# Top-k attention and a leaky-ReLU MLP on one core: the written order of a two-step cycle laid out anew

## The chip, the cores and the metric

The kernel runs on one core of a Trainium2 chip. The metric is the time of one execution in microseconds on the device. TensorE is called PE here, VectorE DVE, ScalarE ACT, GpSimd POOL, and SyncE, which issues most DMAs, SP.

## What is computed

q, k and v are (8, 8, 576, 64) in float32, x is what attention gives, as (4608, 512), w_in is (512, 2048) and w_out (2048, 512).

```python
scores = scale * np.matmul(q, k.transpose(0, 1, 3, 2))
kth = np.partition(scores, -top_k, axis=-1)[..., -top_k:-top_k + 1]   # top_k = 32
scores = np.where(scores >= kth, scores, -1000000000.0)
scores = scores - np.max(scores, axis=-1, keepdims=True)
attn = np.exp(scores)
attn = attn / (np.sum(attn, axis=-1, keepdims=True) + 1e-09)
x = np.matmul(attn, v)             # then (B, H, S, D) to (B*S, H*D)
h = x @ w_in
out = np.maximum(0.01 * h, h) @ w_out
```

## The kernel before

**Units.** Two heads share the 128 partitions, so 64 heads are 32 pairs. A unit is 128 rows of scores for two heads: 128 queries of one pair, or the 64 queries that 576 leaves over, of two pairs. There are 144 units, 18 for each batch. One step of the main loop (L742) begins one unit; two units that follow each other have their scores and their values computed together, in even steps.

**What a unit goes through.** `scores` (L214) multiplies 64x64 tiles on PE into PSUM tiles `wide` (two buffers) and `narrow`, and ACT copies them to `s_sb`. `top_k` (L295) is DVE's work: larger and smaller halves (`pairs`, L302), then four rounds of the eight largest (L307) with three replacements (L312) between; it is a generator that stops at each `yield`, and `slot()` lets it go on. `limits` (L316) makes `nleast` on ACT and `nbias` in two small POOL instructions. `mask` (L326) and `exponents` (L330) are two ACT passes each, `sums` a small ACT instruction that gives `ze`, `reciprocals` (L338) one on DVE that gives `rz`, and `normalize` (L342) two ACT passes more. `transpose` (L345) splits the float32 words into 16-bit halves on POOL (L352, two copies), sends them to DRAM (L353) and reads them back transposed as `wT` (L355), both on SP's queue. The first units and units 14 and 15, called HASTY, are transposed on PE instead (`transpose_in_haste`, L357, and ACT's copies in `keep_transposed`, L368). `weigh_whole` (L385) and `weigh_left` (L401) multiply `wT` with `vt` on PE, and `keep_values` (L413) copies the result to `x`, two copies per unit pair.

**The MLP** is another generator (`mlp`, L491). It takes the tokens in chunks of 256 (two of 128 at first, done by `plain`, L573). For one chunk PE computes eight times a `ph` of two blocks (L510, eight products in all), and ACT makes `gT` of each (L516). The second layer is a 2x2 block product of seven products (L524, L526), eight matmuls each. Some of these read sums that POOL makes (L467): after the fourth and the eighth `ph` three sums are put on a list (s1, s2 and one in g21), and `sum_now` issues what is on the list:

```python
            if f0 % 4 == 3:
                at = slice(f0 - 3, f0 + 1)
                sum_later(s1[:, at, :], g21[:, at, :], g22[:, at, :], ALU.add)
                sum_later(s2[:, at, :], s1[:, at, :], g11[:, at, :], ALU.subtract)
                sum_later(g21[:, at, :], g11[:, at, :], g21[:, at, :], ALU.subtract)
```

The products come in the order g11, g12, s2, s1, g21, g12 again, g22. `keep_sum` (L531) copies each finished sum from PSUM to `o_sb` on ACT, with six buffers. Between the second and the third product `mlp` calls `sum_now()` itself for all that is still on the list.

**What sets the order.** Everything is written in the order of the program, and each engine works in that order; a wait at the head of an engine's queue holds all behind it. `mlp_steps(budget)` lets the MLP's generator go on for so many columns of matmul; `slot_budget` (L648) spreads what is left of a chunk over the steps until the next chunk is ready, with seven such slots a step. A chunk is ready when `attended` is called, after the values of its last unit.

In an even step s the old order is: limits of unit s-1, transpose of unit s-2, mask with a slot between, exponents with `values` (units s-4 and s-3) between the two, the copies of x, `sum_now(3)`, slots, reciprocal and normalize of unit s-1, slots, `scores` of units s+2 and s+3 with their copies, a last slot. The odd step is the same without values and scores. A unit has its top-k in step n, softmax in step n+1, its transpose in step n+2; the pair's values come in step n+4 for even n (`values_at`, L622; one step earlier for HASTY).

Twelve units (26, 27, 34, 35 and the same 36 and 72 later) have their scores computed in the first steps, while PE has little else to do (`score_early`, L668, `EARLY_SCORES`), and kept in DRAM; their even steps have no `scores`.

Of the kernel before, what the change touches and what calls it, by code (L numbers as in the profile page):

```python
# [20 lines left out]
def kernel(  # L21
# [192 lines left out]
    def scores(us):  # L214


        narrow = ps_sc.tile([P, 2, 512], F32, name="narrow")
        ps = {}
        for k, u in enumerate(us):
            wide = ps_sc.tile([P, 2, 512], F32, name="wide", bufs=2)  # L220
            ps[u] = ((wide[:, :, 0:WIDE], 0, WIDE),
                     (narrow[:, :, k * NARROW:(k + 1) * NARROW], WIDE, S))

        order = ((us[0], 0), (us[0], 1), (us[1], 1), (us[1], 0))
        for u, part in order:
            to, k0, k1 = ps[u][part]
            for n in range(0, len(u.quarters), 4):
                for i, pi, side, r0, q0 in u.quarters[n:n + 4]:
                    qt, kt = qk_of[pi]
                    d = slice(side * D, (side + 1) * D)  # L230
                    nc.tensor.matmul(to[r0:r0 + LEFT, i, :], qt[d, q0:q0 + LEFT],  # L231
                                     kt[d, k0:k1], start=True, stop=True)
        for u in us:
            u.both = work.tile([P, 2, S], F32, name="s_sb", bufs=5)
            u.s = [u.both[:, i, :] for i in range(2)]
        for u, part in order:
            to, k0, k1 = ps[u][part]
            nc.scalar.copy(u.both[:, :, k0:k1], to)  # L238
# [106 lines left out]
    def transpose(u):  # L345


        pairs = u.both.rearrange("p i n -> p (i n)").bitcast(U16).rearrange("p (n h) -> p n h", h=2)
        apart = halves.tile([P, 2, 2 * S], U16, name="apart")
        for h in range(2):  # L350
            split = work.tile([P, 2 * S], U16, name="split", bufs=2)
            nc.gpsimd.tensor_copy(split, pairs[:, :, h])  # L352
            nc.sync.dma_start(apart[:, h, :], split)  # L353
        u.wT = work.tile([P, 2 * NKC - 1, P], F32, name="wT", bufs=3)
        nc.sync.dma_start_transpose(out=u.wT.bitcast(U16), in_=apart.rearrange("p h n -> (p h) n"))  # L355
# [57 lines left out]
    def keep_values(pair, po, b, q0):  # L413
        ch, col = x_at(b * S + q0)
        if ch not in x_of:
            x_of[ch] = [xpool.tile([P, CHMAX], F32, name=f"x{c}") for c in range(HP)]
        for side in range(2):
            nc.scalar.copy(x_of[ch][pair % HP + side][:, col:col + po.shape[-1]], po[:, side, :])  # L418
# [6 lines left out]
    def hidden_of_few(ch, x):  # L425

        g_of = {}
        for j in range(NFC // 4):
            ph = ps_ml.tile([P, 512], F32, name="ph", tag="ml")
            for c in range(HP):  # L430
                nc.tensor.matmul(ph, x[c][:, 0:P], w_in[c][:, j * 512:(j + 1) * 512],  # L431
                                 start=(c == 0), stop=(c == HP - 1))
                if c == 1:
                    yield 2 * 512
            g_of[j] = raws.tile([P, 2 * DMODEL], U16, name="scale", bufs=2).bitcast(F32)
            nc.scalar.activation(g_of[j], ph, AF.Prelu, alpha=SLOPE)
            yield 2 * 512
            if j:
                yield from turned(j - 1, g_of)
        few[ch] = g_of  # L440
# [50 lines left out]
    def mlp(ch):  # L491
# [13 lines left out]
        for f0 in range(HALF):  # L505
            ph = ps_ml.tile([P, 2, CHMAX], F32, name="ph", tag="ml")
            for i in range(2):
                f = f0 + i * HALF
                for c in range(HP):
                    nc.tensor.matmul(  # L510
                        ph[:, i, 0:n], w_in[c][:, f * P:(f + 1) * P], x[c][:, 0:n],
                        start=(c == 0), stop=(c == HP - 1),
                    )
                    if c == 1 or i == 0 and c == HP - 1:
                        yield 2 * n
# [102 lines left out]
    LAG = 3  # L618
    HASTY = (*range(8), 14, 15)
    MIDDLE, END = 0, 1  # L620

    def values_at(n):  # L622

        return (n | 1) + LAG - (n in HASTY), MIDDLE

# [3 lines left out]
    EARLY_SCORES = {0: 4, 1: 2, 2: 1, 3: 2, 4: 1, 5: 2}  # L629
# [5 lines left out]
    for n, u in enumerate(steps):  # L635
        ch, _ = x_at(u.b * S + u.q0)
        done_tokens[ch] += u.rows * len(u.pairs)
        if done_tokens[ch] == CHUNKS[ch] * HP:
            ready_at.append((values_at(n), ch))
    assert [ch for _, ch in ready_at] == list(range(len(CHUNKS)))  # L640

    def attended(*place):
        for at, ch in ready_at:
            if at == place:
# [3 lines left out]
    def slot_budget(s):  # L648

        after = [at for (at, _), _ in ready_at if at >= s]  # L650
        until = after[0] if after else s
        if len(after) >= len(CHUNKS) - EARLY:
            return EARLY_SHARE
        return backlog[0] / ((until + 1 - s) * SLOTS)

    EARLY_SHARE = 500
    SLOTS = 7

    with tc.manual_schedule():
# [15 lines left out]
        def load_more(s):  # L675

            at_once = 2
            while len(v_of) < NPAIR:
                n = len(v_of)
                due = values_at(starts[n])[0]  # L680
                if n < LOADED_V:
                    load_v(n)
                elif values_at(last[n - LOADED_V])[0] > s:
# [41 lines left out]
        def values(*place):  # L725
            due = [u for n, u in enumerate(steps) if values_at(n) == place]
            if not due:
                return ()
            po = ps_sc.tile([P, 2, 512], F32, name="wide", bufs=2)
            if len(due[0].pairs) == 1:  # L730
                weigh_whole(due, po, FULL + [QUARTERS])
                return [(due[0], po[:, :, 0:P])]
            for n, u in enumerate(due):
                weigh_left(u, po[:, :, n * LEFT:(n + 1) * LEFT])
            return [(u, po[:, :, n * LEFT:(n + 1) * LEFT]) for n, u in enumerate(due)]

        def keep(weighed, *place):
            for u, po in weighed:
                keep_values(u.pairs[0], po, u.b, u.q0)
            attended(*place)  # L740

        for s in range(len(steps) + LAG + 1):  # L742
            assert s < 7 or not to_keep
            cur, old, older, new = unit(s), unit(s - 1), unit(s - 2), ()
            in_haste = s - 2 in HASTY
            if s % 2 == 0:
                new = [u for u in steps[s + 2:s + 4] if u]
            if new and new[0] in early_units:
                new = ()
            picks = top_k(cur) if cur else iter(())  # L750
            budget = slot_budget(s)

            def slot():
                next(picks, None)

            slot()
# [4 lines left out]
            if older and not in_haste:  # L761
                transpose(older)
            if old:
                mask(old, 0)
            mlp_steps(budget)
            if older and in_haste:
                transpose_in_haste(older)
            if old:
                mask(old, 1)
            slot()  # L770
            if older and in_haste:
                keep_transposed(older)
# [3 lines left out]
            weighed = values(s, MIDDLE)  # L776
            if old:
                exponents(old, 1)
                sums(old)
            keep(weighed, s, MIDDLE)  # L780
# [4 lines left out]
            slot()  # L785
            if s % 2:
                slot()
            if old:
                reciprocals(old)
            mlp_steps(budget)  # L790
            if old:
                normalize(old, 0)
                normalize(old, 1)
            mlp_steps(budget)
            slot()
            slot()
            if unit(s + 3) in early_units:
                fetch_scores(unit(s + 3))
            mlp_steps(budget)
            if new:  # L800
                scores(new)
            score_early(EARLY_SCORES.get(s, 0))
            budget = slot_budget(s + 1)
            mlp_steps(budget)
            load_more(s)
        mlp_steps(1e9)
# [62 lines left out]
```

## Time and profile before

| what | us |
|---|---|
| median of 3 runs | 1463.82 (1461.76 to 1465.31) |
| the profiled execution | 1463.53 |
| its span in the profile | 1461.8 |
| mean granted clock of PE | 0.982 |
| PE, DVE, ACT, POOL busy in 300 to 1300, a mean 100 us | 97.4, 97.4, 74.6, 55.4 |
| DVE's first pairs row of a unit | 60.69 |
| DVE's last one | 1371.90 |

Durations of single instructions are the means of the profile's groups, or rows of its timeline, which merges instructions of one kind that follow each other (x is how many). In a list of waits the columns are: engine, what waited, for whom; the total in us, how often, the longest in us. A timeline row has its start, its duration, engine, line and operation, and in brackets the engine's idle time before it with what ended it. Instructions on PE are pipelined: the mean of one is longer than the distance between two.

The first 100 us convert the weights, which arrive as 64-bit floats. From about 400 us on PE works almost without a pause, and after DVE's last unit at 1381 PE still has the end of one MLP chunk and the whole of the last one.

### The profile page before, as it was taken

Reading aid. Unit: us, or ns where it says so; the run is one execution under the profiler, and the core shown is the slowest. Engines: PE = TensorE matmul, PEld = TensorE weight load, DVE = VectorE, ACT = ScalarE, POOL = GpSimd, SP = SyncE. Lnnn points to the kernel's source line nnn. Section 1 sums busy time; section 2 is a strip of 40 time slices with the busy share of each in tenths; the row PEclk is TensorE's granted clock in tenths of the full one; section 3 lists DMA queues with packets and bytes.
Section 4 is the critical chain, followed back from the end, with each engine's and each line's share of the span. In section 5 each row is a group of like instructions: output and inputs, shape, how many; then the busy total and the mean of one; then the engine's idle time right before and its main releaser. Section 6 shows DMA issues by size and latency. Waiting matters only on the chain.

```text
span 1461.8 us, 27967 instructions
## 1 busy us (share of the span) xinstructions
PE 1373.3 (94%) x9848; PEld 1065.6 (73%) x9850; DVE 1317.9 (90%) x3401; ACT 1058.5 (72%) x2235; POOL 728.6 (50%) x775
## 2 busy tenths in 40 slices
PE   7858988789999999999999999999899999999998
PEld 2335446668787788878788877778788888788887
DVE  7987899999999999999999999999899999999700
ACT  8887777668687878777778786768587877777711
POOL 3213333554646465555556564556465655555622
PEclk9989998999999999999999999999999999999999
DMA  8941154655666546664766557755766455545420
GB/s 328 343 163 50 57 137 117 180 166 141 198 171 173 141 135 190 189 175 137 211 167 180 145 143 190 190 161 151 191 168 174 130 165 143 164 138 145 131 63 15
DMA packets 384445, 232.19 MB, mean 159 GB/s; under 512 B 320944, under 2 KB 331696, under 8 KB 382384
## 3 DMA queue, kind: packets, MB, share of 16 engines
q1 hardware_dynamic: 383728, 229.88, 55.7%
q8 instruction: 77, 1.26, 0.4%
q14 instruction: 64, 0.52, 0.1%
q10 hardware_dynamic: 576, 0.52, 0.1%
HBM read 55.77 MB, written 95.55 MB: 104 GB/s over the span
## 4 chain that ended last, share of the span: by engine, by line
PE 65%; DVE 18%; DMA 7%; ACT 6%; issue 2%; POOL 2%; SPq 0%; ACTq 0%; DVEq 0%; POOLq 0%
PE ph L510 23%; PE pz L526 22%; PE wide L394 9%; DVE tops L307 8%; DVE pairs L312 6%; PE wide L231 4%; DMA wT<-apart 4%; PE narrow L231 2%; PE pz L578 2%; DVE pairs L302 2%; DMA apart<-split 2%; ACT s_sb L238 1%; PE ph L431 1%; DMA vt<-in_vk_dram 1%; ACT s_sb L331 1%
## 5 line engine op out<-in xcount | busy, mean ns | idle before, releaser
L307 DVE MAX8 tops<-pairs 128x8 f32<-128x288 f32 (+1 forms) x1152 | 638.5, 595 | 0.0
L510 PE MATMUL ph<-x,w_in 128*128 128x256 f32 x2176 | 491.7, 383 | 1.6 <-ACT gT L516 1.6
L510 PEld LDWEIGHTS ph<-x,w_in 128*128 128x128 f32 x2176 | 407.4, 190 | 84.0 <-issue 20.8
L312 DVE MATCH_REPLACE8 pairs<-tops,pairs 128x288 f32<-128x288 f32 (+1 forms) x864 | 461.5, 541 | 0.0
L323 POOL TENSOR_TENSOR nbias<-tops 128x2 f32<-128x2 f32 x144 | 107.9, 749 | 574.5 <-DVE tops L307 567.1
L352 POOL COPY split<-s_sb 128x1152 uint16<-128x1152 uint16 x268 | 298.7, 1143 | 8.3 <-ACT s_sb L343 8.3
L343 ACT ACTIVATE s_sb<-s_sb,rz 128x576 f32<-128x576 f32 x288 | 207.3, 768 | 66.9 <-DVE rz L340 66.7
L526 PE MATMUL pz<-w_out,gT 128*128 128x256 f32 x1088 | 245.2, 381 | 0.6 <-ACT o_sb L533 0.6
L526 PEld LDWEIGHTS pz<-w_out,gT 128*128 128x128 f32 x1088 | 205.7, 190 | 31.5 <-issue 2.5
L331 ACT ACTIVATE s_sb<-s_sb,nbias 128x576 f32<-128x576 f32 x288 | 219.3, 764 | 0.9
L328 ACT ACTIVATE s_sb<-s_sb,nleast 128x576 f32<-128x576 f32 x288 | 214.4, 770 | 4.7
L302 DVE TENSOR_TENSOR pairs<-s_sb 128x576 f32<-128x576 f32 x288 | 212.3, 778 | 5.0
L394 PE MATMUL wide<-wT,vt 128*64 128x128 f32 (+1 forms) x2560 | 165.4, 290 | 30.2 <-DMA wT<-apart 21.5
L394 PEld LDWEIGHTS wide<-wT,vt 128*64 128x64 f32 (+1 forms) x2560 | 134.6, 141 | 68.1 <-issue 31.3
L238 ACT COPY s_sb<-wide 128x704 f32<-128x704 f32 x130 | 98.1, 755 | 86.4 <-PE wide L231 86.4
L516 ACT ACTIVATE gT<-ph 128x512 f32<-128x512 f32 x136 | 80.5, 592 | 76.7 <-PE ph L510 76.7
L526 PE MATMUL pz<-raw,top 128*128 128x256 f32 x544 | 125.0, 384 | 0.0
L526 PEld LDWEIGHTS pz<-raw,top 128*128 128x128 f32 x544 | 101.1, 190 | 21.2 <-issue 8.4
L231 PE MATMUL wide<-kt,qt 64*64 64x352 f32 x1040 | 105.0, 474 | 3.6 <-ACT wT L371 2.9
L324 POOL TENSOR_SCALAR nbias<-nbias 128x2 f32<-128x2 f32 x144 | 85.8, 596 | 12.6
L418 ACT COPY x<-wide 128x128 f32<-128x128 f32 (+1 forms) x160 | 32.2, 260 | 74.4 <-PE wide L394 57.9
L533 ACT COPY o_sb<-pz 128x256 f32<-128x256 f32 x119 | 43.8, 368 | 57.1 <-PE pz L526 57.1
(81 smaller groups left out, 1202.1 us busy)
## 6 DMA issues: line engine op xcount, KB each, us to landing
apart<-split SPq DMA_DIRECT2D x268, 288.0 KB, 2.2
raw<-in_weights_dram SPq DMA_DIRECT2D x15, 1024.0 KB, 6.9
vt<-in_vk_dram SPq DMA_DIRECT2D x32, 320.0 KB, 3.9
qt<-in_qT_dram SPq DMA_DIRECT2D x32, 288.0 KB, 3.8
kt<-in_kT_dram SPq DMA_DIRECT2D x32, 288.0 KB, 3.9
out_dram<-o_sb SPq DMA_DIRECT2D x68, 128.0 KB, 3.0
kept<-gT SPq DMA_DIRECT2D x12, 576.0 KB, 4.3
s_sb<-kept SPq DMA_DIRECT2D x12, 576.0 KB, 4.3
```

The lines of the kernel that those rows point to most:

```text
L231: nc.tensor.matmul(to[r0:r0 + LEFT, i, :], qt[d, q0:q0 + LEFT], kt[d, k0:k1], start=True, stop=True)
L238: nc.scalar.copy(u.both[:, :, k0:k1], to)
L302: nc.vector.tensor_tensor(pairs[:, :, n, :], u.both[:, :, 0:HS], u.both[:, :, HS:S], op)
L307: nc.vector.max(out=u.tops[:, i, r, :], in_=rest[i])
L312: nc.vector.match_replace(out=rest[i], in_to_replace=u.tops[:, i, r, :], in_values=rest[i], imm_value=LOWEST)
L328: nc.scalar.activation(u.s[i], u.s[i], AF.Prelu, bias=u.nleast[:, i:i + 1], scale=1.0, alpha=BELOW)
L331: nc.scalar.activation(u.s[i], u.s[i], AF.Exp, bias=u.nbias[:, i:i + 1], scale=SCALE, accum_out=u.z[:, i:i + 1])
L343: nc.scalar.activation(u.s[i], u.s[i], AF.Copy, bias=0.0, scale=u.rz[:, i:i + 1])
L352: nc.gpsimd.tensor_copy(split, pairs[:, :, h])
L394: nc.tensor.matmul(po[n * D:(n + 1) * D, side, 0:P], v_of[u.pairs[0]][k, at, side, :], u.wT[k, at + side * NKC if at + 1 < NKC else at, :] ...
L510: nc.tensor.matmul(ph[:, i, 0:n], w_in[c][:, f * P:(f + 1) * P], x[c][:, 0:n], start=(c == 0), stop=(c == HP - 1),)
L526: nc.tensor.matmul(to, g[:, f, :], w(f), start=(first and f == 0), stop=(f == HALF - 1), skip_group_check=not first)
```

## The change

The order of the program is written for two steps at once, in two functions `even` and `odd`.

- `scores` is cut in three: the PSUM tiles, the matmuls (at the end of the even step, as before) and ACT's copies, which now stand in the following odd step.
- Values of a pair stand beside them, at the end of the even step ahead of the scores. They use 128 columns that the scores leave free in the first `wide` tile. x is one tile for all four blocks, and one ACT copy serves both sides; it stands in the odd step.
- The softmax of a pair's two units is shifted apart. The odd unit has limits, mask, exponents, reciprocal and normalize all in the even step after its top-k. The even unit has limits, mask and exponents in the odd step after its top-k, reciprocal and normalize in the even step after that. In one even step s ACT so normalizes unit s-2 and later unit s-1, and DVE has two reciprocals; in an odd step it has none.
- `transpose` is cut in `split` and `transpose`. Unit s-2 of an even step is split behind its normalize in the same step; in an odd step, right behind limits and mask.
- `sum_now(2)` stands near the end of the even step, `sum_now(3)` behind the copies of the odd one.
- The last two units (142 and 143) join HASTY. `slot_budget` counts 1400 columns for values and scores of an even step (GROUP). `EARLY_SCORES` takes 4, 2, 2, 2, 2 units in steps 0 to 4 in place of 4, 2, 1, 2, 1, 2 in steps 0 to 5.

```diff
@@ keep_values
-        for side in range(2):
-            nc.scalar.copy(x_of[ch][pair % HP + side][:, col:col + po.shape[-1]], po[:, side, :])
+        nc.scalar.copy(x_of[ch][:, pair % HP:pair % HP + 2, col:col + po.shape[-1]], po)
@@
-    LAG = 3
-    HASTY = (*range(8), 14, 15)
+    HASTY = (*range(8), 14, 15, 142, 143)
...
-    EARLY_SCORES = {0: 4, 1: 2, 2: 1, 3: 2, 4: 1, 5: 2}
+    EARLY_SCORES = {0: 4, 1: 2, 2: 2, 3: 2, 4: 2}
@@ slot_budget
-        after = [at for (at, _), _ in ready_at if at >= s]
-        until = after[0] if after else s
+        after = [at for at, _ in ready_at if at > s]
...
-        return backlog[0] / ((until + 1 - s) * SLOTS)
+        until = after[0] if after else s + 1
+        group = [GROUP * (at % 2 == 0 and at < len(steps)) for at in range(s, until)]
+        return max((backlog[0] + sum(group)) / len(group) - group[0], 0.0) / SLOTS
...
+    GROUP = 1400
@@ the steps: these take the place of the loop at L742
+        def even(s):
+            cur, old, older = unit(s), unit(s - 1), unit(s - 2)
+            in_haste = s - 2 in HASTY
...
+            next(picks, None)
+            if older:
+                reciprocals(older)
+            for _ in range(3):
+                next(picks, None)
+            load_waiting()
+            send_now()
+            if old:
+                limits(old)
+                mask(old, 0)
+                mask(old, 1)
+            mlp_steps(budget)
+            if older:
+                normalize(older, 0)
+                normalize(older, 1)
+                if not in_haste:
+                    split(older)
+                    transpose(older)
+                else:
+                    transpose_in_haste(older)
+            mlp_steps(budget)
+            if old:
+                exponents(old, 0)
+                exponents(old, 1)
+                sums(old)
+            if older and in_haste:
+                keep_transposed(older)
+            if old:
+                reciprocals(old)
+            for _ in picks:
+                pass
+            for _ in range(3):
+                mlp_steps(budget)
+            if old:
+                normalize(old, 0)
+                normalize(old, 1)
+            sum_now(2)
+            score_early(EARLY_SCORES.get(s, 0))
+            mlp_steps(budget)
+            mlp_steps(budget)
...
+            ps, spare = tiles_for_scores(new) if new else (None, [])
+            weighed = values(s, spare)
+            if new:
+                scores(new, ps)
+            load_more(s)
+            return new, ps, weighed
+
+        def odd(s, new, ps, weighed):
...
+            for _ in picks:
+                pass
+            send_now()
+            load_waiting()
+            if old:
+                limits(old)
+                mask(old, 0)
+                mask(old, 1)
+            if older and not in_haste:
+                split(older)
+                transpose(older)
+            keep(weighed)
+            if new:
+                keep_scores_of(new, ps)
+            if older and in_haste:
+                transpose_in_haste(older)
+                keep_transposed(older)
+                keep(values(s, []))
+            attended(s)
...
+            sum_now(3)
+            mlp_steps(budget)
+            mlp_steps(budget)
+            if old:
+                exponents(old, 0)
+            mlp_steps(budget)
+            if old:
+                exponents(old, 1)
+                sums(old)
+            for _ in range(4):
+                mlp_steps(budget)
...
```

## The prediction, as put on record

> **What bounds the kernel now.** I read the page's busy shares first, then PE's waits, then the timeline around the longest wait.
>
> ```profile
> PE 1373.3 (94%) x9848; PEld 1065.6 (73%) x9850; DVE 1317.9 (90%) x3401; ACT 1058.5 (72%) x2235; POOL 728.6 (50%) x775
> PE 65%; DVE 18%; DMA 7%; ACT 6%; issue 2%; POOL 2%; SPq 0%; ACTq 0%; DVEq 0%; POOLq 0%
> ```
>
> Two engines are nearly full: PE holds 65% of the chain and DVE follows. A step costs DVE 8.77 us where nothing waits (its rows start at 1301.01 and 1309.79), so eight steps cost 70.2. PE's eight steps, one chunk of the MLP, cost 71.1 in an undisturbed stretch (1053.31 to 1124.42): 120 products of 0.4415 (the page counts each twice; x40 take 8.83), four values groups of 2.28 and four scores groups of 2.1. PE has no slack at all: whatever it waits, the run gets longer by.
>
> PE's waits between 250 and 1390 us, and one of them in the timeline:
>
> ```profile
> PE wide L394 <- DMA wT<-apart: 21.0, 10, 5.4
> PE wide L406 <- DMA wT<-apart: 5.6, 2, 4.5
> PE wide L406 <- DMA vt<-in_vk_dram: 5.1, 4, 1.8
> PE ph L510 <- ACT gT L516: 1.6, 2, 1.0
> PE pz L526 <- ACT o_sb L533: 0.6, 1, 0.6
> ```
> ```profile
> 1030.34 2.23 POOL L352 COPY split<-s_sb 128x1152 uint16<-128x1152 uint16 x2
> 1037.09 0.43 PE L394 MATMUL wide<-wT,vt 128*64 128x128 f32 x2
> 1037.25 2.60 SPq L355 DMA_TRANSPOSE wT<-apart  x1
> 1041.92 3.81 PE L394 MATMUL wide<-wT,vt 128*64 128x128 f32 x38 [4.40 <-DMA wT<-apart]
> ```
>
> The odd unit's weights are split at the start of step n+2, cross two DMAs (4.59 and 4.63 here) and arrive 13.0 us after that step's start at 1028.90; PE wants them at 1037.5. Nothing waits for POOL in that list. That is the point to remember, because the sums that feed the products now run early:
>
> ```profile
> 1016.41 1.27 POOL L467 TENSOR_TENSOR top<-gT 128x512 f32<-128x512 f32 x1 [1.85 <-ACT gT L516]
> 1017.76 1.27 POOL L467 TENSOR_TENSOR top<-top,gT 128x512 f32<-128x512 f32 x1
> 1024.80 7.17 PE L526 MATMUL pz<-raw,top 128*128 128x256 f32 x32
> ```
>
> The second half of s2 is done at 1019.03; PE begins the product that reads it at 1024.80.
>
> The clock is the last view (five-us windows: PE busy in the first pair, PEclk after POOL's pair):
>
> ```profile
> 1035.00:1040.00 5.00, 2.52 (x12) 1.74 (x11) 4.97 (x12) 3.61 (x7) 2.92 (x5) 1.00 0.47 139
> 1040.00:1045.00 5.00, 3.08 (x30) 2.78 (x30) 5.00 (x16) 1.35 (x5) 1.35 (x2) 0.75 0.94 270
> 1045.00:1050.00 5.00, 5.00 (x29) 4.16 (x29) 4.97 (x13) 2.14 (x5) 1.80 (x3) 0.91 0.80 86
> ```
>
> After 4.40 us without work PE runs at 0.75 and 0.91: 3.08 x 0.25 + 5.00 x 0.09 = 1.2 us lost. The waits of 2.87 and 5.36 us lost 1.7 and 2.5 in the same way; after 2.31 the 40 matmuls still took 2.34.
>
> **What goes.** Values move from the middle of the even step to its end, some 4 us later, and the odd unit's transpose now starts in the odd step before, so the DMAs have about 4 us to spare. I strike out the waits of 300 to 1370 us on wT (20.2) and vt (3.4), and with them the clock losses (2.5 + 1.7 + 1.2): at most 29 us. The two copies of x become one: 0.43 against some 0.37 (the 128x256 copy, o_sb), 64 times, about 4 us of ACT, which has slack; I count nothing. Scores no longer share a PSUM tile with values; no wait on that shows in PE's list, so nothing. Values beside scores save a change of shape, under 0.1 us per pair. DMAs are the same apart from the last pair's two transposes and their four halves; v loads are issued after values, with two steps in place of one and a half before they are due: the vt waits go.
>
> **What comes: the sums behind the split.** A chunk's hidden layer ends in an odd step, just after that step's sums were issued. The next place in the order is inside the following even step, where POOL first has split(older), and this now waits for normalize(older), which the change puts in that same step behind limits and both masks. By the written order this holds for 14 chunks (steps 32, 40, ... 136). From the start T of the even step on DVE: pairs, a max and a replace 2.9, reciprocal, so ACT normalizes at T+3.3 (nleast and masks, 1.7, fit before); 1.44 later the split, 2.23, two sums, 2.6: s2 is complete at **T+9.6**. The other limit is PE's own: after scores of the step before (P) come 4 products of the hidden layer and 8 of g11, to P+5.3; then ACT's o_sb 0.37, nleast 0.23, masks 1.44, normalize 1.44, split 2.23, sums 2.6, with handovers **P+13.75**. PE has 12 more products to do and is there at P+10.6. So PE stalls 3.15 us per chunk at the least, more if DVE's T+9.6 comes later. Going through eight steps with these durations, scores end 3.4 us into the odd step before, so T = P+5.3, the sums land at P+14.9 and the stall is 4.3.
>
> Behind the waiting split stand, on POOL, three more sums (1.28, 2.5) and the next nbias, done at T+14.8; the exponents that read it start at T+16.8, so 2 us cover it. On SP the split's DMAs hold back sends and loads of qt, kt by the same 4 us; o_sb has six buffers and loads are due steps later: nothing.
>
> **What is late next.** After the stall four products (1.77), values and scores (4.38) end 6.9 us into step 65 where the stall was in 64. ACT copies the scores, but then waits for o_sb of the third product (P'+7.06) before nleast, masks, normalize and exponents of step 66: ze at P'+12.65. DVE's second reciprocal of step 66, due 7.3 us into it, is 3.5 us late; in step 68, behind gT of the hidden layer, 1.35. So DVE's eight steps become 70.2 + 3.5 + 1.35 = 75.1. Three of the thirteen chunks between steps 32 and 136 have no scores in the stalled step (2.1 less): 13 x 75.1 - 6.3 = 970, where before took 1309.79 - 368.93 = 941: **+29**. PE's own ring gives the same by another way: 13 x (71.1 + 3.15 + 1.2 for the clock) - 5 x 2.1 = 970. Both at their full price, the clock on DVE's ring too: +45, the upper end. With neither clock nor DVE's share, 13 x 74.2 - 10.5 = 954: +13, the lower end.
>
> The Trainium skill ("TensorE: Matmul & The Clock Gate", section "Part 1: The HAM clock gate") has PE at half rate after one idle window of about 3.4 us, until about 3.4 us of work have passed. By it each 4.3 us stall would cost another 1.7 us, 22 us over thirteen chunks, and a stall of 3.15 none; this trace already shows the drop after 2.87.
>
> **The start.** In steps 2 to 9 the hasty transposes stand in ACT's path: in an odd step it now copies scores, then waits for transposes (1.15), copies wT (1.16), waits for values (2.35), copies x, and only then takes the exponents. Before, an exponent (0.77) lay beside the values. I count 1.5 us more for each of four pairs: **+6**. Bounds: -8 (DVE's wait of 8.2 at 131.97 goes and nothing comes) to +14 (every wait of ACT in full, 3.5 a pair).
>
> **The end.** From step 136 on: 300 products (132.5), six values (13.7), three scores (6.3), two more transposes in haste (2.3), changes of shape 1, the stall and clock (5.5), waits for the wT copies and x of the last pair (2.2), the last sums and DMA (3.4): 166.9 from P, that is 161.6 from the step's start; before took 1461.8 - 1309.8 = 152. **+9.6**. The haste saves the split and two DMAs (2.2 + 4.6) of the last pair, but PE has other work then (its waits there were 0.80 and 0.52), so that is worth 1.
>
> Sum against the profiled execution, 1463.53 (span 1461.8; the median is 1463.82): 1463.5 + 29 + 6 + 9.6 = **1508**. EARLY_SCORES ends one step earlier with the same 12 units, and GROUP and SLOTS only place the products; their cost is in the order used above. If the budgets put the end of the hidden layer two slots earlier, the stall would be gone.
>
> **Rivals.**
> - *Only PE's ring counts* (+13), the start gains a little (-3) and the end costs 6: 1480. For it: ACT has 28% free. Against: its waits for PE lie in the same order as the reciprocal.
> - *Faster*: the sums land before PE. Price: the 29 us above, less 2.3 for transposes and 2 at the start: 1439. It decides at one place: o_sb to second sum must take under 5.3 us on PE's clock, where I add up 8.4. For it: DVE's and PE's waits on DMA do go.
> - *Even*: the gain of 24 to 29 and a stall of about 2 us cancel: 1463.
> - *Worse*: the clock is paid on DVE's ring (+45) and ACT falls behind at the start (+14): 1532.
>
> **How the numbers follow.** Forecast 0.60, PE's ring alone 0.13, faster 0.15, even 0.04, worse 0.08. 0.2% is about what a measurement of this kernel can tell from no change. Slower: 0.60 + 0.13 + 0.08 = 0.81; faster 0.15; same 0.04. The range from 1468 to 1532 holds the forecast with its bounds (1480 by PE's ring, less 12 if the start gains its full 8 and the end costs nothing; 1532 above), and leaves out the faster and the even case.
>
> **What would show it.** Right: PE's list of waits gains "pz <- POOL top", about 14 times and 3 to 4.5 us each, next to a POOL row top<-gT that stands behind a split; the granted clock under 1 just after; DVE's wait of rz on ze grows from 30.2 us to 60 or more; no wait on wT<-apart. Wrong: if no PE row waits for POOL, the time is near 1440; if PE waits for POOL and DVE's waits do not grow, near 1480.

## The result and the profile after

| | before | after |
|---|---|---|
| median, us | 1463.78 (1461.76 to 1465.31) | **1545.82** (1544.88 to 1546.06) |
| ratio, 95% interval | | 1.056 [1.0542, 1.0578] |
| the span in the profile, us | 1461.8 | 1543.9 |
| mean granted clock of PE | 0.982 | 0.947 |

The change makes the kernel 82 us slower; 1508 was forecast, and 1532 was the upper end. Cut at DVE's first `pairs` row of steps 32 and 136 (thirteen chunks of the MLP lie between), the spans of all kernels divide so:

| kernel | step 32 begins | steps 32 to 136 | mean chunk | 136 to the end | median |
|---|---|---|---|---|---|
| before | 368.9 | 940.9 | 72.4 | 152.0 | 1463.78 |
| **after** | 377.7 | 1006.5 | 77.4 | 159.6 | 1545.82 |
| 1 sums at the odd step's end | 374.8 | 921.7 | 70.9 | 152.1 | 1450.35 |
| 2 sums with one input | 375.8 | 1006.7 | 77.4 | 160.8 | 1545.0 (one run) |
| 3 sums ahead of split | 373.0 | 936.5 | 72.0 | 152.7 | 1463.72 |
| 4 stall filled, too long | 384.2 | 1074.4 | 82.6 | 182.3 | 1639.59 |
| 5 stall filled | 375.5 | 982.9 | 75.6 | 167.8 | 1530.28 |
| 6 before, two-input work beside pairs | 369.6 | 952.9 | 73.3 | 153.8 | 1478.03 (one run) |
| 7 before, one-input work beside pairs | 375.3 | 955.3 | 73.5 | 154.6 | 1487.11 (one run) |
| 8 exponents first at the start | 380.0 | 1009.0 | 77.6 | 159.6 | 1550.64 |
| 9 is 1 and 8 | 380.1 | 923.1 | 71.0 | 152.1 | 1457.09 |
| 10 is 1, unit 14 not hasty | 371.4 | 925.1 | 71.2 | 151.9 | 1447.19 |
| 11 is 1, last pair not hasty | 375.8 | 923.0 | 71.0 | 154.4 | 1451.45 |
| 12 is 10 with the old early scores | 368.9 | 924.4 | 71.1 | 151.9 | 1448.01 |

So of the 82.1 by which the span grew, 8.8 lie ahead of step 32, **65.7** in the thirteen chunks and 7.6 at the end.

The page of after, its busy shares and its chain by engine:

```profile
PE 1389.3 (90%) x9866; PEld 1089.0 (71%) x9868; DVE 1354.8 (88%) x3401; ACT 1043.0 (68%) x2159; POOL 691.3 (45%) x771
PE 43%; DVE 36%; ACT 10%; issue 6%; POOL 5%; DMA 1%; DVEq 0%; SPq 0%; ACTq 0%; POOLq 0%
```

PE fell from 65% of the chain to 43%; DVE, ACT, POOL and the issue of instructions have what it lost. Such a spread suggests that no engine is the bound by itself, but a ring: a round of work that goes through several engines, each waiting for the one before. The groups of the page (busy, mean ns, idle before them and what ended it) show where the ring waits, first a line of before, then three of after:

```profile
L526 PE MATMUL pz<-raw,top 128*128 128x256 f32 x544 | 125.0, 384 | 0.0
```
```profile
L358 POOL COPY split<-s_sb 128x1152 uint16<-128x1152 uint16 x264 | 294.9, 1145 | 362.0 <-ACT s_sb L349 360.9
L533 PE MATMUL pz<-raw,top 128*128 128x256 f32 x544 | 152.7, 439 | 85.4 <-POOL top L474 85.4
L346 DVE RECIPROCAL rz<-ze 128x2 f32<-128x2 f32 x144 | 22.8, 158 | 96.5 <-ACT ze L342 96.3
```

POOL's split waits for normalize, PE's product for POOL's `top`, DVE's reciprocal for ACT's `ze`. In before no PE row waited for POOL. DVE's waits for `ze` between steps 32 and 136, before and then after:

```profile
DVE rz L340 <- ACT ze L336: 19.6, 14, 4.2
```
```profile
DVE rz L346 <- ACT ze L342: 51.9, 35, 4.1
```

All of DVE's waits in these steps grew from 19.6 to 54.2, and its `pairs` from 154.8 to 181.9: 34.6 and 27.1 of the 65.7. The middle of that ring in the timeline, in the even step 80, which begins at 841.73; first POOL, then PE, then DVE in steps 81 and 82:

```profile
846.37 2.23 POOL L358 COPY split<-s_sb 128x1152 uint16<-128x1152 uint16 x2 [3.78 <-ACT s_sb L349]
848.57 1.27 POOL L474 TENSOR_TENSOR top<-gT 128x512 f32<-128x512 f32 x1
849.91 1.27 POOL L474 TENSOR_TENSOR top<-top,gT 128x512 f32<-128x512 f32 x1
851.14 1.77 POOL L474 TENSOR_TENSOR gT<-gT 128x512 f32<-128x512 f32 x1
```
```profile
843.44 1.89 PE L533 MATMUL pz<-raw,top 128*128 128x256 f32 x8
851.23 5.71 PE L533 MATMUL pz<-raw,top 128*128 128x256 f32 x16 [5.90 <-POOL top L474]
```
```profile
850.59 2.94 DVE L308 TENSOR_TENSOR pairs<-s_sb 128x576 f32<-128x576 f32 x2
871.64 0.17 DVE L346 RECIPROCAL rz<-ze 128x2 f32<-128x2 f32 x1 [2.86 <-ACT ze L342]
```

The split begins 3.78 late, behind normalize. The two sums behind it make s2 complete at 851.18, 9.45 after the step's start. PE had done the first half of the product at 845.3 and stood for 5.90. The 16 rows after the stall took 5.71, where 16 such rows take 3.72 elsewhere (393.28). And `pairs`, which takes 1.43 to 1.45 elsewhere, took 2.94 beside POOL's sums: the forecast has nothing of that. The clock (columns: PE busy, PEld, DVE, ACT, POOL, then PEclk, DMA share, GB/s):

```profile
845.00:850.00 5.00, 0.33 (x2) 0.00 (x0) 5.00 (x15) 4.01 (x10) 3.56 (x4) 0.85 0.26 100
850.00:855.00 5.00, 3.77 (x9) 3.05 (x10) 4.96 (x9) 0.71 (x2) 5.00 (x4) 0.50 0.70 77
855.00:860.00 5.00, 5.00 (x65) 3.93 (x67) 5.00 (x14) 2.04 (x5) 4.13 (x6) 0.97 0.56 170
```

The granted clock is 0.50 for the 3.77 us that PE works between 850 and 855: about 2 us of work lost in this stall (an estimate: half of 3.77, and a little more up to 860).

So three things could make up the 65.7: s2's place in POOL's queue, the clock after the stall, and the slow `pairs`.

### The profile page after: what moved, and what is told of

Same layout as the page of the kernel before. It is cut to its first block, busy times and chain, and to the rows that moved or that the text cites. A ratio compares the mean times of both kernels' runs of the same rounds, so it can differ in the third digit from the quotient of the medians.

```text
span 1543.9 us, 27941 instructions
## 1 busy us (share of the span) xinstructions
PE 1389.3 (90%) x9866; PEld 1089.0 (71%) x9868; DVE 1354.8 (88%) x3401; ACT 1043.0 (68%) x2159; POOL 691.3 (45%) x771
## 4 chain that ended last, share of the span: by engine, by line
PE 43%; DVE 36%; ACT 10%; issue 6%; POOL 5%; DMA 1%; DVEq 0%; SPq 0%; ACTq 0%; POOLq 0%
PE pz L533 19%; DVE tops L313 17%; DVE pairs L318 12%; PE ph L517 11%; PE wide L402 5%; DVE pairs L308 4%; ACT s_sb L349 3%; ACT s_sb L337 3%; PE wide L235 3%; POOL top L474 2%; POOL split L358 2%; PE narrow L235 2%; ACT s_sb L334 1%; DMA raw<-in_weights_dram 1%; PE wide L414 1%
## 5 line engine op out<-in xcount | busy, mean ns | idle before, releaser
L517 PE MATMUL ph<-x,w_in 128*128 128x256 f32 x2176 | 482.7, 381 | 0.7 <-ACT gT L523 0.7
L308 DVE TENSOR_TENSOR pairs<-s_sb 128x576 f32<-128x576 f32 x288 | 247.7, 899 | 11.4 <-ACT s_sb L244 1.8
L533 PE MATMUL pz<-w_out,gT 128*128 128x256 f32 x1088 | 241.2, 379 | 0.0
L329 POOL TENSOR_TENSOR nbias<-tops 128x2 f32<-128x2 f32 x144 | 64.8, 450 | 378.4 <-DVE tops L313 374.5
L533 PE MATMUL pz<-raw,top 128*128 128x256 f32 x544 | 152.7, 439 | 85.4 <-POOL top L474 85.4
L334 ACT ACTIVATE s_sb<-s_sb,nleast 128x576 f32<-128x576 f32 x288 | 207.7, 768 | 4.7
L533 PEld LDWEIGHTS pz<-raw,top 128*128 128x128 f32 x544 | 117.2, 221 | 116.0 <-POOL top L474 91.0
L402 PE MATMUL wide<-wT,vt 128*64 128x128 f32 (+1 forms) x2560 | 158.8, 287 | 9.4 <-ACT wT L379 5.8
L425 ACT COPY x<-wide 128x256 f32<-128x256 f32 (+1 forms) x80 | 26.9, 346 | 126.3 <-PE wide L235 92.4
L346 DVE RECIPROCAL rz<-ze 128x2 f32<-128x2 f32 x144 | 22.8, 158 | 96.5 <-ACT ze L342 96.3
```

The costliest lines, as they stand in the source:

```text
L308: nc.vector.tensor_tensor(pairs[:, :, n, :], u.both[:, :, 0:HS], u.both[:, :, HS:S], op)
L334: nc.scalar.activation(u.s[i], u.s[i], AF.Prelu, bias=u.nleast[:, i:i + 1], scale=1.0, alpha=BELOW)
L402: nc.tensor.matmul(po[n * D:(n + 1) * D, side, 0:P], v_of[u.pairs[0]][k, at, side, :], u.wT[k, at + side * NKC if at + 1 < NKC else at, :] ...
L517: nc.tensor.matmul(ph[:, i, 0:n], w_in[c][:, f * P:(f + 1) * P], x[:, c, 0:n], start=(c == 0), stop=(c == HP - 1),)
L533: nc.tensor.matmul(to, g[:, f, :], w(f), start=(first and f == 0), stop=(f == HALF - 1), skip_group_check=not first)
```

## The experiments

**Theory A**: s2's place behind split is the cause; the stall, and what it does to the clock, travel round the ring to DVE. **Rival C**: POOL's sums and DVE's `pairs` run into each other, and that is the part the forecast missed.

**1. The sums at the end of the odd step.**

```diff
@@ end of odd
             score_early(EARLY_SCORES.get(s, 0))
+            while later and later[0][4] is None:
+                sum_now(1)
             load_more(s)
```

> The changed kernel, with the chunk's sums issued at the end of the odd step, so that POOL has them ahead of the even step's split. Theory A (the sums behind the split are the cause): PE's 14 waits for POOL (85.4 us) go, steps 32 to 136 take 930 to 950 us in place of 1006, the run 1470 to 1490 us. Rival B (two softmaxes of ACT in one even step are too long for DVE's second reciprocal, and PE's wait is only where the slack collects): PE waits elsewhere instead, DVE's waits of rz for ze stay at 50 us in these steps, and the run stays above 1520.

Measured: 1450.35, ratio to before 0.991 [0.9875, 0.9944]. Its waits between steps 32 and 136, PE's two longest and all of DVE's:

```profile
PE pz L533 <- ACT o_sb L540: 11.1, 8, 2.5
PE wide L402 <- DMA wT<-apart: 5.8, 5, 2.8
```
```profile
DVE pairs L308 <- ACT nleast L328: 0.5, 1, 0.5
```

The wait for `top` is gone, and with it DVE's for `ze` (51.9 between the same steps in after, none here); so rival B falls. The gain is larger than theory A had it (930 to 950 in these steps, 1470 to 1490 in all). Twelve of the thirteen chunks take 70.8 to 70.9 us, the other 71.2: the steps are DVE's own work. The undisturbed chunks of before took 70.9 to 71.1 too, but others up to 75.0. So the rest of the change takes 19 us out of these steps, and the place of one trio of sums puts 85 back.

**2. The same sums, with one input each**, so that POOL reads half as much. The additions are left out of s1, s2, g21 and g12.

```diff
@@ sum_now
-            nc.gpsimd.tensor_tensor(to, a, b, op)
+            if to.shape[-1] == P:
+                nc.gpsimd.tensor_scalar(to, a, 1.0, None, ALU.mult)
+            else:
+                nc.gpsimd.tensor_tensor(to, a, b, op)
```

> The changed kernel, with the additions of s1, s2, g21 and g12 left out: POOL multiplies their first input by 1 in the same place, so each has one input in place of two. Theory C (DVE's pairs, which have two inputs, and POOL's two-input sums slow each other): no pair of pairs rows takes over 1.5 us where 2.95 and 2.62 were seen, DVE's pairs fall by about 25 us in steps 32 to 136, PE still waits for POOL 14 times, and the run is near 1515. Rival D (any work of POOL, or the DMAs, slow the pairs): the rows next to the sums stay over 1.8 us and the run near 1540.

Measured: 1545.0, span 1543.2, the chunk still 77.4. Most `pairs` beside a sum are back at their length; the place corresponding to the one above, POOL and then DVE:

```profile
846.92 1.49 POOL L475 TENSOR_SCALAR top<-gT 128x512 f32<-128x512 f32 x1
848.49 1.49 POOL L475 TENSOR_SCALAR top<-top 128x512 f32<-128x512 f32 x1
```
```profile
848.95 1.44 DVE L308 TENSOR_TENSOR pairs<-s_sb 128x576 f32<-128x576 f32 x2
```

Between steps 32 and 136 `pairs` cost 28 us less (181.9 and 153.9), and DVE's waits for `ze` and for copied scores rose by 14 each. So neither theory came whole: most rows are back at their length, as C has it, but the time is near D's. The slow `pairs` are real, but in this kernel they lie in time that DVE would have waited. Rival C falls as the missing part. The sums themselves were a little longer here (1.49 against 1.27), 0.44 for the two that the ring goes through, so a gain of up to 6 us in the thirteen chunks could be hidden here, but not 37.

**3. The two waiting sums ahead of split**, in the same even step.

```diff
@@ even
                 if not in_haste:
+                    sum_now(2)
                     split(older)
```

> The kernel after with one edit: in the even step the two waiting sums (s1 and s2, second halves) stand on GpSimd ahead of the older unit's split, instead of behind it and the younger unit's normalize. Nothing else moves. Theory A (what costs is s2's place behind split): s2 is then complete about 4 to 5 us after the even step's start on VectorE instead of 9.6, TensorE is there about then, the wait of pz for top falls from 85.4 to under 15, and the time to 1450 to 1465, near the 1450 of the version with the sums at the end of the odd step. Rival C (what costs is that pairs and GpSimd's sums run into each other): the sums move from the odd step's pairs to the even step's, so that as many pairs are slow, and the time stays above 1530. Rival D (split delayed by the sums makes transposed weights late): waits of wide for wT<-apart rise by over 20 in all and the time lies between, 1480 to 1520.

Measured: 1463.72, ratio to before 1.0004 [0.9986, 1.0021]. PE, POOL and DVE in step 40, which begins at 444.89:

```profile
448.88 1.99 PE L533 MATMUL pz<-raw,top 128*128 128x256 f32 x8 [1.57 <-POOL top L474]
```
```profile
445.71 1.76 POOL L474 TENSOR_TENSOR top<-gT 128x512 f32<-128x512 f32 x1
447.55 1.27 POOL L474 TENSOR_TENSOR top<-top,gT 128x512 f32<-128x512 f32 x1
449.53 2.23 POOL L358 COPY split<-s_sb 128x1152 uint16<-128x1152 uint16 x2 [0.71 <-ACT s_sb L349]
```
```profile
453.75 2.85 DVE L308 TENSOR_TENSOR pairs<-s_sb 128x576 f32<-128x576 f32 x2
```

One added line, which puts two sums ahead on one queue, takes 82 us off: s2 is done 3.9 after the step's start and PE waits 1.57, after which its 8 rows take 1.99 (the clock holds). Between steps 32 and 136 DVE does not wait for `ze` at all. The chunk is 72.0, and 70.9 in run 1. Here the slow `pairs` are not hidden: one in each chunk takes 2.84 to 2.86, and 1.76 to 1.78 in run 1, a difference of 1.1, which is the difference of the chunks. So rival C's contention is real, but worth 1.1 a chunk here. Rival D's transposes are not late (7.4 us of waits).

**4 and 5. Is the clock on the ring?** Matmuls that nobody reads fill part of the stall.

```diff
@@ product, run 5 (run 4: fill=20, and into pz)
-        def product(to, g, w, first=False):
+        def product(to, g, w, first=False, fill=0):
             for f in range(HALF):
+                for k in range(fill if f == 4 else 0):
+                    nc.tensor.matmul(pa[:, COLS:2 * COLS], g11[:, k % HALF, :], w_at(k % HALF, 0),
+                                     start=True, stop=True, skip_group_check=True)
...
-        yield from product(px, s2, of("t2"))
+        yield from product(px, s2, of("t2"), fill=10)
```

> The kernel after, with 20 more matmuls of 128x256 in each chunk, put on TensorE ahead of the half of the product with s2 that it waits for (their sums are never read). At 0.22 us each they fill about 4.4 of the 6.1 us of each of the 14 stalls, so that some 2 us of idle time are left. Theory A' (the forecast's ring through s2, its missing part being the clock, which makes the work after each stall 2.0 us longer on the ring that VectorE waits for): the matmuls after a stall go at full rate (16 in 3.6 us, not 5.7), the idle time before them falls to about 2, the chunk from 77.4 to about 75.4, and the time to about 1518 (26 to 28 off), with VectorE's waits for ze down by as much. Rival (the clock is a by-product, the ring is longer for another reason, as pairs slowed down by GpSimd): the matmuls go at full rate but wait as much later on, and the time stays within 5 of 1546. If the fillers reach past the stall, s2's product starts late and the time goes above 1546.

Run 4 measured 1639.59 and tells nothing of the clock: the profile counts each product twice, so 20 of them are 8.8 us, and they waited for ACT's copy of the sum beside them (45.4 us in 14 waits). They were longer than the stall.

> The kernel after with fillers again, mended in two places: 10 products of 128x256 in each chunk (20 rows of the profile at 0.22 us, 4.4 us in all) instead of 20 (40 rows, 8.8 us: more than the stall), and into the unused half of the PSUM bank that the product with s2 goes to, so that they wait for no copy of ScalarE (the first fillers did, 45.4 us in 14 waits). Their sums are never read. Each lies in a stall of about 6.1 us and leaves some 1.7 idle. Theory A' (the clock after a stall, 2.0 us of each, is on the ring): the matmuls after a stall go at full rate (16 rows in 3.6 to 3.7, not 5.7), the chunk goes from 77.4 to about 75.4, the wait of pz for top to about 20 to 30 in all, and the time to 1518 to 1522. Rival (the clock is off the ring): full rate after the stalls, the chunk stays at 77 and the time within 5 of 1546.

Run 5 is for the time alone: its fillers go to the bank of PSUM in which the product with s2 is being added up, and its output is no longer right. Measured: 1530.28, ratio to before 1.0471 [1.0448, 1.0493]. The fillers and the products after them, in the chunk shown above; then the clock:

```profile
834.25 4.48 PE L534 MATMUL pz<-w_out,gT 128*128 128x256 f32 x20
840.76 3.72 PE L536 MATMUL pz<-raw,top 128*128 128x256 f32 x16 [2.04 <-POOL top L474]
```
```profile
840.00:845.00 5.00, 4.24 (x26) 3.54 (x28) 4.96 (x11) 2.17 (x5) 5.00 (x4) 1.00 0.57 120
845.00:850.00 5.00, 5.00 (x72) 3.73 (x69) 5.00 (x14) 2.58 (x6) 3.68 (x6) 1.00 0.31 118
```

The 16 rows take 3.72 and not 5.71, the clock is 1.00, and the chunk goes from 77.4 to 75.6: **23.7 us** over the thirteen chunks, with 22.4 less of DVE's waits for `ze`. So the clock was on the ring, and the rival falls.

Not every stall was mended. In steps 32 to 136 two of thirteen still have the low clock behind them: at 385.00, after 3.23 us idle, and in the stall of step 56, after the same 2.04 us that did no harm above:

```profile
612.92 5.41 PE L536 MATMUL pz<-raw,top 128*128 128x256 f32 x16 [2.04 <-POOL top L474]
```

By the granted clock each of the two loses 1.7 us, so the clock's whole part in after is nearer 27 than 23.7 (an estimate).

The time fell by 15.5 and not by the expected 24 to 28, as the end grew by 8.2: there are 17 such products and 14 stalls, and fillers that meet no stall are added work (argued from the counts).

**6 and 7. The contention by itself, in the kernel before**: POOL work that nobody needs, right beside `pairs`.

```diff
@@ limits, run 6
         nc.gpsimd.tensor_tensor(u.nbias, least_kept, largest, ALU.subtract)
+        nc.gpsimd.tensor_tensor(scratch, w_in[0][:, 0:384], w_in[1][:, 0:384], ALU.add)
         nc.gpsimd.tensor_scalar(u.nbias, u.nbias, SCALE, None, ALU.mult)
@@ limits, run 7
+        for k in range(2):
+            nc.gpsimd.tensor_copy(scratch, w_in[k][:, 0:384])
```

> The kernel before, with one more POOL addition of two inputs (128x384) in every step, just where DVE begins its pairs. Nothing reads it. Theory C: pairs rise from 1.43 to 2.2 or more per step, and the run by 80 to 140 us. Rival D: as the one-input version of the same length, and rival E (what slowed the pairs was something else): pairs stay at 1.43 and the run within 10 us of 1464.

> The kernel before, with two POOL copies of one input (128x384) in the same place as the addition of the run with two inputs. Nothing reads them. Theory C: pairs stay near 1.43 to 1.5 and the run within 15 us of 1464. Rival D (any POOL work beside them): pairs over 2 us and the run over 1540.

Measured: 1478.03 and 1487.11, one run each. In neither did `pairs` become longer (155.0 in steps 32 to 136, and 154.8 in before), so the numbers of theory C and of rival D did not come. A place in run 6, DVE's row and POOL's:

```profile
802.97 1.43 DVE L303 TENSOR_TENSOR pairs<-s_sb 128x576 f32<-128x576 f32 x2
```
```profile
803.02 0.76 POOL L324 TENSOR_TENSOR nbias<-tops 128x2 f32<-128x2 f32 x1 [4.19 <-DVE tops L308]
803.74 1.52 POOL L325 TENSOR_TENSOR scratch<-w_in,w_in 128x384 bf16<-128x384 f32 x1
```

Here POOL began after DVE, and POOL was the one held up: a 128x2 instruction took 0.76, and takes 0.20 where no `pairs` runs. In after, a sum was already under way when `pairs` began, and `pairs` was held up. The Trainium skill ("SBUF — State Buffer", "Who interferes with whom") has this as a rule: VectorE with two inputs in SBUF and a GpSimd instruction that reads SBUF share a port pair, and whichever starts first keeps it for its whole instruction. These rows agree (2.94 where POOL was first, 0.76 where DVE was), but not run 2's: there a one-input sum was under way as 33 `pairs` began, and 21 of them still took 1.43 to 1.45, the other 12 1.54 to 1.88. The same 33 took 1.79 to 2.96 in after. No run varied the order alone. These two runs became slower by another way: the added work stands between the two instructions that make `nbias`, for which the exponents then wait (27.3 us on run 6's page, under 1 in before; DVE's wait for `ze` between steps 32 and 136 went from 19.6 to 31.3 and 34.0, and these steps became 12.0 and 14.5 longer).

**8 and 9. The start: the order of the odd step.** In hasty odd steps (`ahead`) the exponents go ahead of, and among, the transposes.

```diff
@@ odd
             if older and in_haste:
                 transpose_in_haste(older)
+                if ahead:
+                    exponents(old, 0)
                 keep_transposed(older)
-                keep(values(s, []))
+                weighed = values(s, [])
+                if ahead:
+                    exponents(old, 1)
+                    sums(old)
+                keep(weighed)
...
-            if old:
+            if old and not ahead:
                 exponents(old, 0)
...
```

> The kernel after with one edit: in odd steps with a hasty unit (the start, and units 14 and 15) the exponents and their sums are issued on ScalarE and VectorE ahead of, or among, the hasty transposes and copies, instead of behind them. The kernel after reaches step 32 at 377.7, 8.8 later than before. Theory A (the forecast's start: six of those steps pay for the odd step's order, about +6): step 32 begins 4 to 9 earlier, at 369 to 374, and the time falls as much, to 1537 to 1542. Rival (the start is late because of loads and TensorE's sums of the weights, not of this order): step 32 begins within 2 of 377.7 and the time stays at 1544 to 1548.

> Both edits at once: the second trio of sums issued at the end of the odd step, and the exponents of the start's odd steps ahead of the hasty transposes. The first alone gave 1450.35. If the two gains are independent, as theory A has it (one is in the steady steps, one before step 32), the time is 1450 less what the second edit gives alone, 4 to 9: 1441 to 1446. If the start's gain is taken back by the first chunk's stalls (rival), it is within 2 of 1450.

Measured: 1550.64, 1.0593 [1.0568, 1.0618], and 1457.09, 0.9951 [0.9934, 0.9968]. Step 32 begins 2.3 later than in after, and 5.3 later than in run 1, and the times are 4.8 and 6.7 longer: neither the gain of theory A nor the unchanged time of the rivals. With the order that the forecast blamed undone, the start is no earlier but later, so its reason is not borne out. What that order costs by itself is not shown, as the edit also puts the transposes' copies behind an exponent.

**10, 11 and 12. The start and the end by the lists**: on run 1, HASTY without 14 and 15; HASTY without 142 and 143; and run 10 with EARLY_SCORES as before.

```diff
@@ run 10, and 12
-    HASTY = (*range(8), 14, 15, 142, 143)
+    HASTY = (*range(8), 142, 143)
@@ run 11
-    HASTY = (*range(8), 14, 15, 142, 143)
+    HASTY = (*range(8), 14, 15)
@@ run 12 besides
-    EARLY_SCORES = {0: 4, 1: 2, 2: 2, 3: 2, 4: 2}
+    EARLY_SCORES = {0: 4, 1: 2, 2: 1, 3: 2, 4: 1, 5: 2}
```

> The version with the sums at the end of the odd step (1450.35), with units 14 and 15 no longer hasty: their weights go through split and the transposing DMA, and their values come a step later. That version reaches step 32 at 374.8, 5.8 behind before, and 5 to 6 of it arise in steps 18 and 19, where TensorE waits 8.5 us for the normalized weights in the hasty transposes. Theory (that wait under the shifted order is the start's loss): the wait goes, step 32 comes 3 to 6 earlier, time 1444 to 1448. Rival (the haste feeds the first chunks of the MLP, and TensorE has too little to do without it): step 32 no earlier, or later, and time 1450 to 1458.

> The version with the sums at the end of the odd step (1450.35), with units 142 and 143 no longer hasty, as before the change. The forecast priced this edit at about 1 us of gain at the end. From step 143 to the end it takes 87.8 there, and 90.1 in the kernel before, so up to 2.3 of gain can be the edit's: time 1451 to 1453. Rival (the haste costs TensorE's transposes as much as it saves in DMA): within 1 of 1450.

> Three edits on the kernel after: the second trio of sums at the end of the odd step, units 14 and 15 no longer hasty (these two together gave 1447.19), and the early scores spread over steps 0 to 5 as before the change (4, 2, 1, 2, 1, 2) instead of 4, 2, 2, 2, 2 in steps 0 to 4. The version without the third edit begins step 16 at 228.2, where the kernel before begins it at 221.4, and most of that arises in steps 4 to 11. Theory (the early scores, put one step earlier on TensorE and ScalarE, are the start's loss): step 16 comes 3 to 6 earlier, and the time is 1441 to 1445. Rival (the hasty transposes wait for normalize, which now stands in their own step, and the place of the early scores is indifferent): step 16 within 1.5 of 228.2 and time 1446 to 1449.

Measured: 1447.19, 0.9899 [0.9881, 0.9918]; 1451.45, 0.9929 [0.9909, 0.9949]; 1448.01, 0.9896 [0.9869, 0.9923]. From run 1 to 10 to 12 step 32 comes forward (374.8, 371.4, 368.9, the last as in before), but the steps after it give about 3 us back, and the times of runs 1, 10 and 12 can't be told apart. Run 10's numbers are those of its theory; run 12's are not (step 16 came 2.2 earlier and not 3 to 6, and the time is the rival's). Run 11's end is 2.3 longer in the profile, as its theory has it; its time is within the uncertainty of run 1's. Why the gain at the start is given back was not settled.

Runs 1, 10 and 12 beat both kernels, by about 1% of before.

## Why the prediction was off

**Right**: the direction, the one mechanism that decides, its place and its count. Fourteen PE waits for `top`, behind a split that waits for normalize; s2 complete at T+9.45 in all fourteen (forecast T+9.6); PE there at P+10.6 (measured 845.3 - 834.71 = 10.6). The signs that it named came only in part. The stalls are 5.1 to 6.6 us, not 3 to 4.5. DVE's wait for `ze`, counted from 250 to 1390 us as the 30.2 was, grew to 54.5 and not to 60; the 96.3 on the page is of the whole run. PE's waits for transposed weights fell from 14.8 to 0.6 between steps 32 and 136. The gains were right in kind too: in run 1 PE's waits for transposed weights and `vt` between these steps are 6.4 in place of 18.2.

The end, 159.6, was forecast as 161.6, but that is partly luck. Run 1's end is 152.1 and that of before 152.0, so all of the loss, 7.5, goes with the place of the sums; the forecast gave 5.5 to the stall and its clock and 4.1 to the rest.

**Wrong**: the size of "So DVE's eight steps become 70.2 + 3.5 + 1.35 = 75.1", 970 for the thirteen chunks where 1006.5 were measured. This sum has nothing for the clock. The 36.5 between them divide so:
- **The clock, 23.7** (run 5 against after; some 27 with the two stalls that run 5 left). The forecast had it at 1.2 a stall on PE's own ring alone, and on DVE's only in the upper end. But the products after the stall stand ahead of the values and scores that ACT and DVE wait for: whatever lengthens them lengthens DVE's ring. It costs 1.8 a chunk in time by run 5. The 1.2 was also read too low: the window with clock 0.75 begins with 1.92 us in which PE had no work, and the 38 matmuls after the wait took 3.81, where 38 at full rate took 2.34 (after the wait of 2.31). The Trainium skill ("TensorE: Matmul & The Clock Gate", "Part 1: The HAM clock gate") has half rate for some 3.4 us after an idle window of about 3.4 us. The forecast worked 22 us for thirteen chunks out of it, an estimate, and left it out of the sum. The runs agree with the half rate (clock 0.50) and nearly with the sum (23.7), but not with the length of the idle time: the clock also fell after 2.87 us in before, and after 2.04 in the stall of step 56 of run 5.
- **The eight steps without waits, 9.1**: 70.2 was eight times one row; a chunk in which nothing waits takes 70.9 in before and in run 1 alike. 13 x 0.7.
- **The rest, 3.8**: run 5's 982.9 less 13 x 70.9 is 61.2, where the forecast had 970 - 13 x 70.2 = 57.4. The two stalls left in run 5 are 3.4 of this. The sum is so nearly right, but not what fills it: only 30.7 of the 61.2 are waits of DVE, and most of the other half is slow `pairs`, which the forecast did not have. Run 2 shows that DVE would have waited in their place.

The stall itself was 5.9 at step 80, not 4.3. The scores of the step before ended 3.0 into that step and not 3.4, and the step took 9.97 and not 8.77, its `pairs` being slowed to 2.62; so T was P+7.0 and not P+5.3. DVE's deadline counts, and 9.45 + 7.0 - 10.6 = 5.9. The ring goes through s2, and how long PE has stood there before it adds nothing to the ring; what it adds is the lower clock behind it.

**The start**, +6, was +8.8, but not for the reason given: runs 8 and 9 take that away and step 32 comes later still. Of the 8.8, 2.9 go with the early sums (run 1), 3.4 with units 14 and 15 (run 10) and 2.5 with the early scores (run 12). Each is a difference of two single profiles, and after and run 5, the same program up to there, begin step 16 at 226.0 and 224.0; so these shares are not shown beyond some 2 us.

**The faster rival** was the right picture of the rest of the change. With the sums ahead of PE the forecast gave 1439, and runs 1 and 3 gave 1450 and 1464. In run 1 the thirteen chunks gain 19.2, where it counted at most 29; the start loses 5.9, where it counted a loss of 2; the end loses nothing, where it counted 2.3. Its condition (o_sb to second sum in under 5.3 us) is what those runs fulfil by moving the sums.

## What to carry to other kernels

When a step is moved, go through each queue it now stands in and ask what small instruction is behind it: here two sums of 1.27 us behind a split that waits cost 95 us against the same sums issued at the end of the step before. A stall that is long enough to lower PE's clock costs more than its own length, and what it adds belongs in the ring of whoever waits for the work after it, not in PE's alone. Read that cost from the rows behind the stall, not from a window that is partly idle. Take an undisturbed period from a whole period of the trace, not from one step times eight.

## What the runs showed of the chip that was not expected

- After 2.04 us idle PE's clock stayed at 1.00 at 840.76 in run 5, and fell at 612.92 in the same run, where 16 rows took 5.41 and not 3.72. After the 14 idle times of 5.1 to 6.6 us in after it fell every time; at step 80 the work behind took about 2.0 us longer. So at 2 us the length of the idle time alone did not decide it, and what did is open.
- DVE's `pairs` (two inputs, 128x576) and POOL's two-input instructions hold each other up: `pairs` went from 1.43 to 2.85 and 2.94 when a POOL sum was under way, and stayed at 1.43 to 1.45, in 21 of 33 cases, beside one-input work of the same size; when `pairs` was first, a 128x2 instruction of POOL took 0.76 in place of 0.20. This contention cost nothing where DVE waited anyway (run 2) and 1.1 us a chunk where it did not (run 3).
